# Ten of sixteen normalized tiles turned by DMA, the bias row loaded early, and eight banks for the first sums

## The chip, the cores and the metric

One core of one Trainium2 chip. The metric is the device time of one execution in microseconds (us), which is what all times below are. The matmul engine TensorE is called PE, VectorE DVE, ScalarE ACT, GpSimd POOL; SP issues most of the DMA transfers (in the kernel before all but 17 of the listed issues; the page lists no busy time for it).

A line of the profile's page called PEclk gives the clock granted to PE in tenths of full speed. Each execution also has a mean granted clock. In the profiled executions of the two kernels half clock (0.50) comes in stretches of 3.4 us or of twice that (in the kernel before from 50.3 to 57.1); both have a mean of 0.979. One stretch of 3.4 us takes about 0.011 off the mean (half of 3.4 is 1.7 us, of a span of 157 to 164), so by this estimate a mean of 1.000 says "no such stretch", 0.989 "one", 0.979 "two, or one of double length". This reading turns out to matter. An execution counts as slow here when it is over 1.5% above the fastest of the same kernel in its group of runs, otherwise as fast; only fast ones enter the ratios.

## The reference

```python
x  = A_x                                   # 1 x 2048 x 640, bf16
xn = layernorm(x)                          # over the 640
A  = irfft2(rfft2(xn) * (w_r + 1j * w_i))  # filter weights: 2048 x 321 each
B  = gelu(xn @ w1 + b1) @ w2 + b2          # w1 640 x 1536, w2 1536 x 640
return x + A + B
```

Two branches start from xn. The spectral one (A) is built from small matmuls with tables, of lengths 128, 16 and 160. The dense one (B) multiplies the transposed xn (xnT) with w1.

## The kernel before

The kernel is a list of operations with priorities; a scheduler in the program places them on engines by an estimate of their times, and the resulting order per engine is fixed at build time. Waits between engines are semaphores. Names that the argument needs: `xn` is a normalized tile of 128 rows (16 tiles in 8 pairs); `T` in the profile is the buffer that holds it; `ps` is PSUM, of which the program uses eight banks; `gT` the activated first-layer result; `gtab`, `etab`, `getab`, `htab`, `mtab`, `ntab` are tables; `Wf` holds the filter weights; `W` in the profile is w1 or w2: matmuls of `xnT,W` read w1, those of `W,gT` read w2 (W2 in the text), and of the loads `W<-in_B_w_dram` the ones after the first 10 us are those of W2. (DVE's `W` is an output buffer.)

How a tile was turned: five PE transposes into PSUM, then a copy. `BYDMA` is empty, so the DMA branch was not used:

```python
BYDMA = ()
...
if c in BYDMA:
    K.op([("sp", 1.6)], 0, lambda ...: e.dma_start_transpose(
         xnT[:, :, 128*c:128*c+128], xnv(n, 0, [[1, D]])), reads=[B_xn, xn], writes=[B_xnT[c]], ...)
    continue
tps = Buf(f"tps{c}", psum, 1, ZONE["tps"])
def xt(e, _, ...):
    for j in range(5):
        ins = e.transpose(psb(tps.slot, ...)[:, 128*j:128*j+128], xnv(n, 128*j, [[1, 128]]), ident[:])
...
K.op([("dve", 0.41), ("act", act_us(640))], pr, copy(... xnT <- tps ...))
```

SP's loads, in the order in which they were issued (the order of the text, which the scheduler in the program kept for SP):

```python
# x tiles, w1, tables G, E, M, N  [cut]
for ri, wsrc in enumerate((A_w_r, A_w_i)):      # 34 filter pieces
    ...  load_w(wsrc, p0, off, m1, 8, 1)  ...
load(W2[:], w2v, B_w2, F * D * 2)               # 1920 KB, one load
load(getab[:], const["GE"], B_ge, 204800)
load(htab[:]..., const["H"], B_h, 524288)
load(b2bc[:], ... b2 broadcast to 128 partitions ..., B_b2b, 163840)   # last
```

The program makes an instruction on SP wait for its inputs before it is issued, and everything behind it on SP waits too:

```python
for o in self.order[name]:
    for d in o.waits:
        e.wait_ge(d.sem, d.count)
    ins = o.emit(...)
```

## Time and profile before

| | before, profiled execution | before, other executions |
|---|---|---|
| time | 162.6 | 158.38, 159.2, 160.29 |
| span of the core | 160.8 | – |
| mean granted clock | 0.979 | not used in the prediction; see the experiments |
| PE busy | 148.7 (92%) | |
| PE's longest wait | 3.91, on activations behind the bias row b2bc | |

The last two rows are read in the prediction, with their lines. What the prediction does not show is where SP put W2, the second layer's weights. This is the timeline of SP in the kernel before (start, length, engine, line, operation, how many):

```profile
36.43 0.59 SPq L469 DMA_DIRECT2D W<-in_B_w_dram  x1
```

W2 is first read by PE at 60.04. It was issued 23.6 us ahead of need; the reader should keep that number.

### The profile page before, as it was taken

The numbers are of one execution on the slowest core, as the hardware profiler recorded it, in microseconds if no ns is written. First come the engines' busy times: TensorE is split into PE (matmuls) and PEld (weight loads), VectorE is DVE, ScalarE is ACT, GpSimd is POOL, SyncE is SP. The second block draws the span as 40 slices with busy tenths as digits, with TensorE's granted clock in tenths as the row PEclk, the third lists the DMA queues.
The fourth block names the chain that finished last, engine by engine and source line by source line (L and its number), as shares of the span: only waits on it lengthen the run. The fifth ranks groups of instructions, "written<-read, shape, count | busy, mean of one in ns | idle before, by whom it ended". The sixth has DMA issues, their size and how long they took to land.

```text
span 160.8 us, 4316 instructions
## 1 busy us (share of the span) xinstructions
PE 148.7 (92%) x1823; PEld 98.4 (61%) x1845; DVE 113.2 (70%) x258; ACT 84.0 (52%) x147; POOL 26.2 (16%) x33
## 2 busy tenths in 40 slices
PE   7979999999981999998999999998999999999994
PEld 7969899999850356464465355443447664665563
DVE  1659999999993024589995786991206999998222
ACT  3288989899709655353246884356865451211000
POOL 1112101111027600302113045202006000000000
PEclk9999999999997589999999999999999999999999
DMA  5999995458941940051649509996651914222112
GB/s 143 356 380 394 212 140 121 105 128 202 378 189 20 207 99 4 4 84 34 131 81 161 90 4 156 208 166 126 138 115 18 167 64 161 86 86 82 41 56 66
DMA packets 30394, 21.71 MB, mean 135 GB/s; under 512 B 12712, under 2 KB 28200, under 8 KB 30376
## 3 DMA queue, kind: packets, MB, share of 16 engines
q1 hardware_dynamic: 23320, 15.39, 38.4%
q0 software_dynamic: 6400, 5.24, 20.2%
q10 hardware_dynamic: 656, 0.82, 1.4%
q8 instruction: 14, 0.23, 0.6%
q14 instruction: 4, 0.03, 0.1%
HBM read 13.58 MB, written 2.62 MB: 101 GB/s over the span
## 4 chain that ended last, share of the span: by engine, by line
PE 57%; SPq 22%; DMA 8%; DVE 4%; ACT 4%; issue 3%; DVEq 0%
PE ps L474 57%; SPq L469 22%; DMA b2bc<-in_B_b_dram 6%; DVE T L723 2%; DMA XV<-U 2%; ACT gT L656 2%; ACT Wf L485 1%; DVE Z L727 1%; ACT xnT L803 1%; DVE Y L486 1%; DVEq L359 0%; ACT U L485 0%; DVE X L824 0%; DVE W L835 0%; SPq L748 0%
## 5 line engine op out<-in xcount | busy, mean ns | idle before, releaser
L474 PE MATMUL ps<-xnT,W 128*128 128x256 bf16 (+2 forms) x413 | 57.8, 294 | 6.0 <-ACT gT L656 4.6
L474 PE MATMUL ps<-W,gT 128*128 128x128 bf16 (+3 forms) x382 | 55.2, 292 | 1.6 <-issue 1.3
L474 PEld LDWEIGHTS ps<-xnT,W 128*128 128x128 bf16 x420 | 35.8, 99 | 23.2 <-ACT gT L656 6.3
L656 ACT ACTIVATE gT<-ps,b1col 128x256 bf16<-128x256 f32 (+2 forms) x84 | 39.7, 506 | 8.8 <-PE ps L474 6.8
L474 PEld LDWEIGHTS ps<-W,gT 128*128 128x128 bf16 x396 | 29.8, 98 | 23.3 <-issue 2.4
L826 POOL DMA_DIRECT2D xnT<-in_A_x_dram x8 | 12.3, 1785 | 33.0 <-ACT xnT L803 23.5
L567 DVE BATCH_NORM_STATS2 stats<-X 128x6 f32<-128x320 bf16 x32 | 14.3, 472 | 2.9 <-DMA X<-in_A_x_dram 2.9
L485 ACT ACTIVATE Wf<-ps 128x960 bf16<-128x960 f32 (+1 forms) x9 | 7.6, 878 | 15.5 <-PE ps L474 15.5
L723 DVE TENSOR_TENSOR T<-Y,Wf 128x1288 bf16<-128x1288 bf16 x16 | 12.4, 821 | 0.8 <-issue 0.8
L572 POOL TENSOR_TENSOR rstd<-ve,mhalf 128x2 f32<-128x2 f32 (+1 forms) x9 | 6.3, 699 | 38.1 <-DVE ve L571 38.1
L485 ACT ACTIVATE Xb<-ps 128x960 bf16<-128x960 f32 (+1 forms) x7 | 7.9, 1157 | 8.0 <-PE ps L474 7.8
L826 POOL DMA_DIRECT2D X<-in_A_x_dram x8 | 7.0, 873 | 27.1 <-DVE X L824 25.6
L485 ACT ACTIVATE XV<-ps 128x1280 bf16<-128x1280 f32 (+1 forms) x8 | 9.3, 1157 | 2.9 <-PE ps L474 2.7
L835 DVE TENSOR_TENSOR W<-ps,xnT 128x640 bf16<-128x640 f32 x8 | 6.5, 819 | 5.6 <-PE ps L474 5.4
L485 ACT ACTIVATE Y<-ps 128x644 bf16<-128x644 f32 x8 | 5.7, 707 | 8.5 <-PE ps L474 8.5
L486 DVE CAST Wf<-ps 128x960 bf16<-128x960 f32 (+1 forms) x3 | 3.1, 1044 | 8.6 <-PE ps L474 8.6
L486 DVE CAST Y<-ps 128x644 bf16<-128x644 f32 x8 | 6.6, 825 | 3.6 <-PE ps L474 3.6
L622 DVE TENSOR_TENSOR T<-T 128x512 bf16<-128x512 bf16 (+1 forms) x32 | 8.5, 315 | 0.0
L486 DVE CAST Xb<-ps 128x960 bf16<-128x960 f32 (+1 forms) x5 | 5.5, 1098 | 4.1 <-PE ps L474 4.1
L485 ACT ACTIVATE U<-ps 128x512 bf16<-128x512 f32 (+1 forms) x12 | 4.6, 435 | 7.1 <-PE ps L474 4.6
L835 DVE TENSOR_TENSOR W<-ps,X 128x640 bf16<-128x640 f32 (+2 forms) x10 | 6.7, 683 | 1.9 <-PE ps L474 1.9
L474 PE MATMUL ps<-getab,XV 32*128 32x160 bf16 (+1 forms) x128 | 7.6, 242 | 0.0
(47 smaller groups left out, 147.7 us busy)
## 6 DMA issues: line engine op xcount, KB each, us to landing
xnT<-in_A_x_dram POOLq DMA_DIRECT2D x8, 320.0 KB, 4.9
X<-in_A_x_dram POOLq DMA_DIRECT2D x8, 320.0 KB, 5.1
out_dram<-W SPq DMA_DIRECT2D x15, 160.0 KB, 1.8
X<-in_A_x_dram SPq DMA_DIRECT2D x7, 320.0 KB, 10.2
W<-in_B_w_dram SPq DMA_DIRECT2D x1, 1920.0 KB, 9.7
Wf<-in_A_w_r_dram SPq DMA_DIRECT2D x15, 80.2 KB, 9.3
Wf<-in_A_w_i_dram SPq DMA_DIRECT2D x15, 80.2 KB, 2.6
W<-in_B_w_dram ACTq DMA_DIRECT2D x1, 800.0 KB, 5.2
```

The lines of the kernel that those rows point to most:

```text
L469: return K.op([(q, 0.45)], 400, lambda e, _: e.dma_start(dst, src), reads=reads, writes=[buf], after=after, nbytes=nbytes, rate=rate)
L474: ins = e.matmul(o_, lhsT=lw, rhs=rh, start=st, stop=sp_, skip_group_check=True)
L485: return e.activation(dst(), src(), ACT.Copy, scale=scale)
L486: return e.tensor_copy(dst(), src())
L567: K.op([("dve", 0.393)], pr, lambda e, _, c=c, h=h: e.bn_stats(stats[:, c, 6 * h:6 * h + 6], view(X, c * D + H2 * h, [[1, H2]])), reads=[B ...
L572: K.op([("pool", 0.65)], pr, lambda e, _, a=a, b=b: e.tensor_tensor(out=rstd[:, a:b], in0=ve[:, a:b], in1=mhalf[:, a:b], op=ALU.pow), read ...
L622: ring_ops.append(K.op([("dve", dve_us(4 * w, 2))], pr, lambda e, _, op=op, x1v=x1v, xfv=xfv, o_=o_, o0=o0, o1=o1, w=w: e.tensor_tensor(ou ...
L656: K.op([("act", act_us(128 * nt, 1))], pr + PRIO["gelu"], lambda e, _, c0=c0, nt=nt, fc=fc, hps=hps: e.activation(gT[:, fc, 128 * c0:128 * ...
L723: filt_ops.append(K.op([("dve", dve_us(4 * KP, 2))], pr, lambda e, _, k=k, Y=Y, TB=TB, pair=pair: e.tensor_tensor(out=view(TT, TB.slot * 8 ...
L727: K.op([("dve", dve_us(2 * KP, 2))], pr, lambda e, _, TB=TB, Z=Z, r=r, op=op: e.tensor_tensor(out=view(Zb, Z.slot * 4 * KP + r * KP, [[2 * ...
L826: K.op([("pool", 1.5)], 51, lambda e, _, c=c, xov=xov, shaped=shaped: e.dma_start(xov(0, D), shaped(xv[:, c, :]), accum_op=ALU.add), reads ...
L835: K.op([("dve", dve_us(w))], 95, lambda e, _, os_=os_, fps=fps, o0=o0, w=w, xov=xov, shaped=shaped, base=base: e.tensor_tensor(out=shaped( ...
```

## The change

Its intent: take transposes off PE and their copies off DVE, close the hole at 48 to 52 us, and let the first sums use all eight banks. To get the DMA transposes out in time, SP may now take its loads by estimated time instead of by place in the text. The core of the diff:

```diff
-                if e == "sp":
-                    t, o = min(cands, key=lambda c: c[1].seq)
-                    if o is not min((p for p in pend[e] if not p.done), key=lambda p: p.seq):
-                        continue
-                else:
-                    t0 = min(c[0] for c in cands)
-                    ...
+                t0 = min(c[0] for c in cands)
+                ...
-BYDMA = ()
+BYDMA = tuple(range(6, 16))
+WLATE = (9.0, 0.9)
+W2LATE = (30.0, 4.0)
+EARLY = 4
@@ loads
+        load(b2bc[:], ..., B_b2b, 163840)             # now ahead of the filter pieces
-                 B_w, 16 * 642 * n, after=[wpad], rate=165e3)
+                 B_w, 16 * 642 * n, after=[wpad], rate=165e3, late=WLATE[0] + WLATE[1] * len(B_w.writers))
-        load(W2[:], w2v, B_w2, F * D * 2)
-        load(getab[:], const["GE"], B_ge, 204800)
-        load(htab[:]..., const["H"], B_h, 524288)
-        load(b2bc[:], ..., B_b2b, 163840)
+        for j in range(4):
+            load(W2[:, 3*j:3*j+3, :], w2v[:, 3*j:3*j+3, :], B_w2, 3*128*D*2, late=W2LATE[0] + W2LATE[1] * j)
+        load(getab[:], const["GE"], B_ge, 204800, late=60.0)
+        load(htab[:]..., const["H"], B_h, 524288, late=62.0)
@@ first-layer sums
-                hps = Buf(f"hps{bi}_{fc}", psum, 1, ZONE["hps"])
+                hps = Buf(f"hps{bi}_{fc}", psum, 1, ZONE["hps"] + (ZONE["bps"] if bi < EARLY else []))
```

The `late` values are hints to the scheduler (not before this time by its own estimate); no wait of the hardware comes from them. All four pieces of W2 write one buffer, `B_w2`, so the first product that reads W2 waits for all four.

More of the change, by code (lines that the diff above doesn't have):

```diff
@@ L248, in schedule @@
                     continue
-                if e == "sp":
-                    t, o = min(cands, key=lambda c: c[1].seq)
-                    if o is not min((p for p in pend[e] if not p.done), key=lambda p: p.seq):
-                        continue
-                else:
-                    t0 = min(c[0] for c in cands)
-                    near = [c for c in cands if c[0] <= t0 + 0.03]
-                    if e == "pe" and self.mode != "128":
-                        near = [c for c in cands if c[0] <= t0 + HOLD and c[1].alts and c[1].alts[0][0][0] == self.mode] or near
-                    t, o = min(near, key=lambda c: (-c[1].prio, c[1].seq))
+                t0 = min(c[0] for c in cands)
+                near = [c for c in cands if c[0] <= t0 + 0.03]
+                if e == "pe" and self.mode != "128":
+                    near = [c for c in cands if c[0] <= t0 + HOLD and c[1].alts and c[1].alts[0][0][0] == self.mode] or near
+                t, o = min(near, key=lambda c: (-c[1].prio, c[1].seq))
                 if best is None or t < best[0]:
@@ L466, in bass_parallel_sum__spectral_gfnet__dense_activation_gelu__prompt_kernel, with load @@
         p_yo, p_y2, p_yf, p_os = Pool(2), Pool(1), Pool(2), Pool(4)
-        def load(dst, src, buf, nbytes, after=(), reads=(), rate=395e3, q="sp"):
-            return K.op([(q, 0.45)], 400, lambda e, _: e.dma_start(dst, src), reads=reads, writes=[buf], after=after, nbytes=nbytes, rate=rate)
+        def load(dst, src, buf, nbytes, after=(), reads=(), rate=395e3, q="sp", late=0.0):
+            return K.op([(q, 0.6 if buf is B_w else 0.45)], 400, lambda e, _: e.dma_start(dst, src), reads=reads, writes=[buf], after=after, nbytes=nbytes, rate=rate, late=late)
         def mms(lst):
@@ L529, in bass_parallel_sum__spectral_gfnet__dense_activation_gelu__prompt_kernel @@
         load(ntab[:], const["N"], B_n, 49152, rate=70e3)
+        load(b2bc[:], bass.AP(tensor=b2v.tensor, offset=b2v.offset, ap=[[0, 128], [1, D]]), B_b2b, 163840)
         WP = 32 * KP
@@ L547, in bass_parallel_sum__spectral_gfnet__dense_activation_gelu__prompt_kernel @@
                             load_w(wsrc, p0 + 1, off + 2 * KP, 127, 7, -1)
-        load(W2[:], w2v, B_w2, F * D * 2)
-        load(getab[:], const["GE"], B_ge, 204800)
-        load(htab[:].rearrange("p a b -> p (a b)"), const["H"], B_h, 524288)
-        load(b2bc[:], bass.AP(tensor=b2v.tensor, offset=b2v.offset, ap=[[0, 128], [1, D]]), B_b2b, 163840)
+        for j in range(4):
+            load(W2[:, 3 * j:3 * j + 3, :], w2v[:, 3 * j:3 * j + 3, :], B_w2, 3 * 128 * D * 2, late=W2LATE[0] + W2LATE[1] * j)
+        load(getab[:], const["GE"], B_ge, 204800, late=60.0)
+        load(htab[:].rearrange("p a b -> p (a b)"), const["H"], B_h, 524288, late=62.0)
         B_b1ps, B_b1c = Buf("b1ps", psum), Buf("b1col")
@@ L599, in bass_parallel_sum__spectral_gfnet__dense_activation_gelu__prompt_kernel @@
                 if c in BYDMA:
-                    K.op([("sp", 1.6)], 0, lambda e, _, c=c, n=n, xnv=xnv: e.dma_start_transpose(xnT[:, :, 128 * c:128 * c + 128], xnv(n, 0, [[1, D]])),
-                         reads=[B_xn, xn], writes=[B_xnT[c]], nbytes=163840, rate=150e3)
+                    K.op([("sp", 1.25)], 500, lambda e, _, c=c, n=n, xnv=xnv: e.dma_start_transpose(xnT[:, :, 128 * c:128 * c + 128], xnv(n, 0, [[1, D]])),
+                         reads=[B_xn, xn], writes=[B_xnT[c]], nbytes=163840, rate=180e3)
                     continue
@@ L747, in bass_parallel_sum__spectral_gfnet__dense_activation_gelu__prompt_kernel @@
                     q = 2 * pair + qq
-                    K.op([("sp", 1.3)], 0, lambda e, _, q=q, qq=qq, U=U, uv=uv: e.dma_start_transpose(
+                    K.op([("sp", 1.25)], 500, lambda e, _, q=q, qq=qq, U=U, uv=uv: e.dma_start_transpose(
                         XV[:, :, 128 * q:128 * q + 128], uv(U, D * qq, [[1, D]])), reads=[U, B_u], writes=[B_v[q]], nbytes=163840, rate=180e3)
```

## The prediction

> **What bounds the kernel now.** I read the page's slices first, then the chain of work that ended last, then the timeline around the hole that these two point at, and last a table of stretches in the steady part before it.
>
> The slices (one digit is the busy share of 4.02 us; the third line is the granted TensorE clock):
>
> ```profile
> PE   7979999999981999998999999998999999999994
> DVE  1659999999993024589995786991206999998222
> PEclk9999999999997589999999999999999999999999
> DMA  5999995458941940051649509996651914222112
> ```
>
> The reader is to see that PE is at nine tenths nearly everywhere: the kernel is bound by TensorE, so that time is won only by taking work off PE or by filling its holes. There is one hole, in slices 12 and 13 (48 to 52 us, digits 8 and 1), and the clock falls to 7, 5, 8 right there and nowhere else.
>
> The chain, at that place (start, length, what):
>
> ```profile
> 37.06 0.91 SPq L469
> 37.97 0.04 issue
> 38.01 0.48 SPq L469
> 38.53 9.79 DMA b2bc<-in_B_b_dram
> 48.34 0.74 ACT xnT L803
> 49.08 0.58 ACT gT L656
> ...
> 51.49 6.30 PE ps L474 x23
> ```
>
> Everything before 38.5 us in this chain is SP issuing one load after another; the broadcast bias row b2bc is the last of SP's 55 loads. It takes 9.79 us to land, ACT waits for it, the activations queued on ACT behind it wait with it, and PE waits for those. The timeline gives the sizes (last bracket: idle before, and what ended it):
>
> ```profile
> 48.34 0.74 ACT L803 ACTIVATE xnT<-b2bc 128x640 f32<-128x640 bf16 x1 [4.44 <-DMA b2bc<-in_B_b_dram]
> 51.49 5.73 PE L474 MATMUL ps<-xnT,W 128*128 128x512 bf16 x13 [3.91 <-ACT gT L656]
> 57.02 0.78 PE L474 MATMUL ps<-gtab,T 128*128 128x128 bf16 x10
> ```
>
> PE is idle for 3.91 us. The table of stretches shows what it costs afterwards (PE busy with its count, granted clock, DMA share, GB/s):
>
> ```profile
> 50.65:57.05 6.40, 5.56 (x14) 0.50 1.05 154
> ```
>
> The 13 matmuls of 512 columns start at 51.49 and the next group at 57.02: 5.53 us, 0.425 us each. In the fast part (34 such matmuls from 112.50 to the next group at 120.06) one takes 0.222 us. The half clock so costs 5.53 - 13 x 0.222 = 2.6 us on top of the 3.9.
>
> The steady part before the hole (PE, PEld, DVE, ACT, POOL, clock, DMA share, GB/s):
>
> ```profile
> 30.70:35.90 5.20, 5.20 (x60) 4.78 (x58) 5.20 (x19) 4.50 (x9) 0.69 (x1) 1.00 0.48 112
> ```
>
> 5.2 us is the period of one pair of x tiles. PE and DVE are both full, and ACT is at 4.5 of 5.2. The DMA rings are half used, while SP is issuing filter weights at about 0.6 us each.
>
> [...] 3.91 us idle, then 0.50 from 50.65 to about 57.0. [...] the activations behind the bias copy stood still for 4.44 us although the sums they were to read had been finished. [...] b2bc, 160 KB, took 9.8 us behind 1920 KB of W2 and 512 KB of H; the transposes that the kernel already makes land in 2.6/3.3/7.4 us (least, median, most). [...] Here a DMA transpose does five blocks at once for about 1.3 us of SP's time (medians 1288 to 1906 ns), and five blocks on PE take 0.28 us plus a copy of 0.48 us on DVE.
>
> **The change part by part.**
>
> Bias row early: no instruction is added; one load of 0.53 us moves from place 55 to just before the filter weights. It would be issued near 9.8 us instead of 38.5 and land long before ACT wants it at 44. Both the hole (3.9 us) and the half clock after it (2.6 us) should go: 6.5 us, all on PE, all on the path.
>
> Ten tiles turned by DMA: it takes 50 transposes off PE. From the timeline a pair's ten start at 31.32 and the next group at 31.88: 0.56 us a pair, five pairs, 2.8 us off the bounding engine. It also takes ten copies xnT<-ps off DVE: a pair's two cost 0.89 us, so 4.4 us in all, and DVE's period falls from 5.2 to about 4.3 us from the fourth pair on. It adds ten DMA transposes to SP: 10 x about 1.3 = 13 us of issuing. SP now issues from 9.8 to 36.4 the 34 filter pieces, 26.6 us; with the ten the stretch ends about 13 us later, near 50, and filter weights are first read at 69 (perhaps 59 after the change). So SP's work stays hidden, narrowly. The transposes' latency of about 3 us, 7 at worst, replaces about 1.5 us of PE transpose plus copy. The first sums lag behind the normalization: the 512-column sums of tiles 8 to 11 start about 44 us, while tile 11 was normalized at about 36. Eight microseconds of slack; hidden.
>
> Eight banks for the first four blocks of sums: PE waited 0.70 us for ACT at 9.64 us with all four banks full. More banks let it run on; ACT is the bound there (8.57 of 10 us in 10 to 20), so I count 0.5 us.
>
> W2 in four pieces, E and H tables late: bytes are unchanged, first use of W2 is 60 us. I count 0.
>
> Sum in the profiled execution: 3.9 + 2.6 + 2.8 + 0.5 = 9.8 us of 160.8. As PE is full elsewhere and its remaining work is the same, work put off from the early part (the first sums, whose share in the shorter pair period shrinks) fills later places, where PE would otherwise have waited or done the same work anyway.
>
> **The rivals.**
>
> (a) The hole is smaller outside the profile. The profiled execution took 162.6 us and the three others 158.38 to 160.29, median 159.2: 3.4 us less. If that difference sits in the landing of b2bc[...], only 9.8 - 3.4 = 6.4 us are there to win: 152.8. If the profile stretches all evenly, it is 159.2 x (1 - 9.8/160.8) = 149.5. The spread of 1.9 us among the three speaks for a part that varies; nothing in one profile decides it.
>
> (b) SP or the DMA rings become the wait. The transposes stand in order with filter pieces whose landing takes up to 12 us early on (the stretch at 0 to 20 us has DMA shares of 0.86 and 1.09), and each waits on SP for its normalization, holding what follows it. Against it: by 25 us, when the first is issued, the later filter pieces land in 2.6 us and the share is 0.5. Should one miss, PE loses 1 to 3 us: 152 to 154. [...]
>
> (c) ACT becomes the bound. With a pair period of 4.3 us ACT has 1.24 us of XV copy and needs 0.49 us for each 256-column activation, while PE makes one such sum in 0.54 us. In 4.3 us ACT can serve 6.2 sums, which with the 0.56 us of PE's own G product keeps PE busy 3.9 of 4.3 us. That could cost up to 0.4 x 4 = 1.6 us. But the scheduler may hand XV copies to the relieved DVE. I count it as part of the range.
>
> (d) The middle chain (width transform, filter, inverse, turned by SP) does not follow. Its start, the last G product, moves from 57.0 to about 46. PE has first and second layer work to fill it, as now (PE waits of 0.1 to 0.5 us between 60 and 120). If the chain stretched to its old end, the gain would be only some 3 us: 156. Against it, DVE, its other engine, has about a fifth of its time free between 60 and 110.
>
> **Range and chances.** The mean of the two readings of (a) is 151.2; I predict 151.3 us. Low end: all of 9.8 and a bit of the clock's variation, 148.3. High end: the smaller hole and 2 us of (b) or (c), 154.8. The 2% line is 156.0. To miss it, (b) or (d) must take nearly everything; I give 0.07 to within 2% and 0.01 to slower, 0.92 to faster.
>
> **What would show it.** In the profile after: no ACT wait on b2bc and no clock digit below 9 after the start; 30 PE transposes instead of 80, 6 copies xnT<-ps instead of 16; a DVE pair period of 4.2 to 4.5 us from about 25 us; the last G product at 46 to 48 us; PE's busy time some 5 us lower (2.8 of transposes, 2.6 of slow clock), and no PE wait over 1 us from 10 us on. Wrong would be: PE waiting for an xnT transpose or on activations held up by another load; SP reaching the last filter piece after the first filter product wants it; a second drop of the clock; or a before-kernel that shows no hole when not profiled, so that the gain is 3 us short.

## The result

| | before | after |
|---|---|---|
| median of the four runs of each taken side by side | 158.79 (156.84 to 160.29, 4 runs) | 162.62 (162.60 to 165.45, 4 runs) |
| ratio of fast runs | 1 | 1.0306 (95%: 1.0209 to 1.0404): slower |
| mean clock of the runs | not on record for these four; 1.000 in most others (see e5) | 0.979, in one of six 0.989 |
| profiled execution: span | 160.8 | 163.7 |
| profiled execution: PE busy / idle | 148.7 / 12.1 | 146.6 / 17.1 |

The ratio here and below is the mean time of one kernel's fast runs over that of the other's fast runs of the same rounds, so it is not quite the ratio of the two medians. Predicted were 151.3 us and a gain; the kernel lost 3%. Both profiled executions are slow ones of their kernel with the same mean clock, 0.979. They are compared below to find the places where time goes; what each place costs in fast runs is taken up with the experiments.

The slices of the kernel after (one digit for 4.09 us; PE, DVE, granted clock, DMA):

```profile
PE   7979999989899819999999999999199959999994
...
DVE  1659999999932574489669859552067899598222
...
PEclk9999999999999996999999999999959999999999
DMA  5999996969999990052773799599800772302112
```

The hole at 48 to 52 us is gone, but there are two new ones: slices 13 and 14 (counted from 0; 53 to 61 us, digits 8 and 1) and slice 28 (115 to 119 us, digit 1). After each of them the clock dips (6; 5). The DMA line stands at 9 from slice 9 to slice 14 (37 to 61 us) and falls to 0 when the first hole ends, so transfers were under way all through it. The waits of PE (total, times, longest) name the two holes:

```profile
PE ps L472 <- DMA W<-in_B_w_dram: 3.9, 1, 3.9
...
PE ps L472 <- DMA XV<-U: 3.3, 1, 3.3
...
PE ps L472 <- DVE W L834: 1.6, 1, 1.6
```

The first waits for W2. Why W2 is late stands in SP's timeline after:

```profile
10.61 11.91 SPq L467 DMA_DIRECT2D Wf<-in_A_w_r_dram  x17
22.57 1.16 SPq L467 DMA_DIRECT2D Wf<-in_A_w_i_dram  x1
26.10 2.62 SPq L599 DMA_TRANSPOSE xnT<-T  x2
28.76 2.54 SPq L467 DMA_DIRECT2D Wf<-in_A_w_i_dram  x4
...
47.33 2.70 SPq L599 DMA_TRANSPOSE xnT<-T  x2
50.07 1.87 SPq L467 DMA_DIRECT2D Wf<-in_A_w_i_dram  x3
51.99 2.19 SPq L467 DMA_DIRECT2D W<-in_B_w_dram  x4
```

From 26.1 to 54.2 us SP is never free: ten transposes (15.3 us together, 1.3 to 2.5 each) and 16 filter pieces (10.1 us, about 0.6 each) alternate, and W2 stands behind all of them. Before that SP stood idle from 23.7 to 26.1, because the first transpose waits for its tile to be normalized (DVE normalizes the pair from 25.63 to 26.43, the transpose is issued at 26.10). W2 is issued at 51.99, where before it was issued at 36.43: 15.6 us later. The scheduler in the program had put these four loads at 47.3 to 48.6 and their landing at 54.0 by its own estimate. The chain of work that ended last (start, length, what) shows the landing, and the same pattern at the second hole:

```profile
53.69 6.88 DMA W<-in_B_w_dram
...
60.61 4.62 PE ps L472 x36
...
113.82 4.75 DMA XV<-U
...
118.61 1.23 PE ps L472 x14
```

PE's timeline after (last bracket: idle before, and what ended it) gives the sizes, and one prediction that came true:

```profile
47.45 0.72 PE L472 MATMUL ps<-gtab,T 128*128 128x128 bf16 x10
...
60.61 2.84 PE L472 MATMUL ps<-W,gT 128*128 128x512 bf16 x12 [3.86 <-DMA W<-in_B_w_dram]
...
118.61 1.23 PE L472 MATMUL ps<-getab,XV 128*128 128x160 bf16 x16 [3.29 <-DMA XV<-U]
```

The last G product starts at 47.45, where it started at 57.02 before: 9.6 us of lead, as the prediction wanted (46 to 48). Then PE reaches the first product with W2 at 60.61 - 3.86 = 56.75, and stands. The table of stretches for what follows the two holes (length; PE busy and count, PEld, DVE, ACT, POOL; clock, DMA share, GB/s):

```profile
60.61:66.80 6.19, 6.03 (x48) 3.87 (x50) 2.67 (x6) 1.52 (x2) 0.00 (x0) 0.72 0.10 38
...
118.61:123.50 4.89, 4.55 (x44) 3.08 (x45) 2.61 (x5) 1.39 (x2) 0.00 (x0) 0.65 0.00 0
```

6.03 us busy at a clock of 0.72 are 6.03 x 0.28 = 1.7 us lost; 4.55 us at 0.65 are 1.6 us. So the balance between the two profiled executions closes:

| term of PE's time | us |
|---|---|
| hole of the bias row gone: idle / half clock after it | -3.9 / -2.6 |
| 50 transposes gone | -2.8 |
| wait for W2: idle / half clock after it | +3.9 / +1.7 |
| wait for the last XV transposes: idle / half clock | +3.3 / +1.6 |
| wait for DVE W, late | +1.6 |
| sum | +2.8 |
| measured, 163.7 - 160.8 | +2.9 |

The gain came, 9.3 us of it; new waits, two of them of the same two-part kind as the one removed, took back 12.1. This is the balance of two slow executions. The fast runs differ by more (1.0306 is some 4.8 us), because the usual execution of the kernel before has less of the hole that was removed (e5).

### The profile page after: what moved, and what is told of

It reads as the page before. It is cut to its first block, busy times and chain, and to the rows that moved or that the text cites. A ratio compares the mean times of both kernels' runs of the same rounds, so it can differ in the third digit from the quotient of the medians.

```text
span 163.7 us, 4234 instructions
## 1 busy us (share of the span) xinstructions
PE 146.6 (90%) x1774; PEld 96.5 (59%) x1795; DVE 111.8 (68%) x252; ACT 80.8 (49%) x143; POOL 26.2 (16%) x33
## 2 busy tenths in 40 slices
DMA packets 37162, 23.35 MB, mean 143 GB/s; under 512 B 19480, under 2 KB 34968, under 8 KB 37144
## 4 chain that ended last, share of the span: by engine, by line
PE 74%; DMA 11%; ACT 4%; DVE 3%; SPq 3%; issue 3%; DVEq 0%; ACTq 0%
PE ps L472 73%; DMA XV<-U 5%; DMA W<-in_B_w_dram 4%; DMA xnT<-T 2%; SPq L467 2%; ACT gT L655 1%; PE ps L606 1%; ACT L655 1%; ACT XV L483 1%; DVE W L834 1%; SPq L747 1%; ACT Wf L483 1%; DVE XV L484 1%; DVE U L484 1%; SPq L599 1%
## 5 line engine op out<-in xcount | busy, mean ns | idle before, releaser
L472 PE MATMUL ps<-W,gT 128*128 128x512 bf16 (+3 forms) x385 | 56.9, 296 | 6.5 <-DMA W<-in_B_w_dram 3.9
L472 PE MATMUL ps<-xnT,W 128*128 128x256 bf16 (+2 forms) x411 | 56.5, 288 | 3.5 <-ACT gT L655 1.1
L472 PEld LDWEIGHTS ps<-xnT,W 128*128 128x128 bf16 x420 | 34.6, 98 | 18.3 <-issue 2.8
L655 ACT ACTIVATE gT<-ps,b1col 128x256 bf16<-128x256 f32 (+2 forms) x84 | 38.6, 509 | 10.3 <-PE ps L472 9.2
L483 ACT ACTIVATE Wf<-ps 128x960 bf16<-128x960 f32 (+1 forms) x8 | 6.8, 870 | 23.2 <-PE ps L472 23.2
L483 ACT ACTIVATE Xb<-ps 128x960 bf16<-128x960 f32 (+1 forms) x8 | 8.7, 1121 | 12.9 <-PE ps L472 12.7
L825 POOL DMA_DIRECT2D X<-in_A_x_dram x8 | 8.0, 996 | 30.6 <-DVE X L823 29.5
L484 DVE CAST Wf<-ps 128x960 bf16<-128x960 f32 (+1 forms) x4 | 4.3, 1072 | 8.7 <-PE ps L472 8.7
L472 PEld LDWEIGHTS ps<-getab,XV 32*128 32x128 bf16 (+1 forms) x128 | 6.9, 147 | 5.3 <-DMA XV<-U 3.8
L823 DVE TENSOR_TENSOR X<-ps,b2bc 128x640 f32<-128x640 f32 x7 | 5.7, 817 | 3.7 <-PE ps L472 3.7
```

Of the source, the lines that this page charges most:

```text
L472: ins = e.matmul(o_, lhsT=lw, rhs=rh, start=st, stop=sp_, skip_group_check=True)
L483: return e.activation(dst(), src(), ACT.Copy, scale=scale)
L484: return e.tensor_copy(dst(), src())
L655: K.op([("act", act_us(128 * nt, 1))], pr + PRIO["gelu"], lambda e, _, c0=c0, nt=nt, fc=fc, hps=hps: e.activation(gT[:, fc, 128 * c0:128 * ...
L823: kept_ops.append(K.op([("dve", dve_us(D))], 30, lambda e, _, kps=kps, xov=xov, shaped=shaped: e.tensor_tensor(out=xov(0, D), in0=shaped(p ...
L825: K.op([("pool", 1.5)], 51, lambda e, _, c=c, xov=xov, shaped=shaped: e.dma_start(xov(0, D), shaped(xv[:, c, :]), accum_op=ALU.add), reads ...
```

## The experiments

Two theories stand. (I) SP's in-order issuing: the ten transposes, with their issue time and their waits for normalized tiles, push W2 (and what else is behind them) past its need; remedy that, and the predicted gain is there. (II) The DMA engines: the transposes, and the accumulating loads that the early bias row moved to 27 to 46 us, fill the DMA engines (their share in 20 to 50 us is 1.02 in the kernel after, 0.67 in the kernel before), so that W2 would be late wherever SP issued it. A third question is what the bias row's hole was worth in executions that were not the slow profiled one.

### e1: only the bias row early, on the kernel before

```diff
+        # SP's order: the load of b2bc ahead of the first filter piece; all else as it was
+        sp = K.order["sp"]; moved = [o for o in sp if B_b2b in o.writes]; ...
+        K.order["sp"] = rest[:at] + moved + rest[at:]
```

> The kernel before with one thing changed: SP issues the bias row ahead of the filter pieces; the order on every other engine is the same. My theory of the hole in the kernel before (3.9 us idle and 2.6 us at half clock, all from that one load): no idle time over 1 us on TensorE near 48 us, no clock below 1.0 there, and 6.5 us less, a ratio of 0.96 (152 us). Rival 1, the hole is mostly an effect of profiling: about 3 us less, 0.98. Rival 2, what is filled there is lost later, as the changed kernel suggests: within 1 us of the kernel before, 1.00.

Measured: 155.49 (155.44 to 155.77), ratio 0.9887 (0.9854 to 0.9919), mean clock 1.000 in all four. No wait of PE over 1.0 us is left in the profile: SP issues the row early, and PE runs its 13 matmuls without the wait and at full clock (SP's timeline, then PE's):

```profile
9.36 0.54 SPq L469 DMA_DIRECT2D b2bc<-in_B_b_dram  x1
```

```profile
47.34 2.98 PE L474 MATMUL ps<-xnT,W 128*128 128x512 bf16 x13
```

So the mechanism is right: one load moved closes the hole. But the gain is 1.1%, some 1.8 us, not 6.5. The same kernel was run again later, on another chip (e14):

> The kernel before with only the bias row moved, once more on the same chip as the two runs before it, to compare them: 155.5 us, ratio 0.989, clock 1.000.

gave 155.45 (155.37 to 155.73), ratio 0.9862 (0.9825 to 0.9900).

### e5: the kernel before once more

Unchanged, for a profile of an undisturbed execution.

> The kernel before, unchanged, for another look with the profile: of seven runs of it beside the last experiments five had a mean clock of 1.000 and two had 0.989. If the run is one of the common kind: TensorE still waits for the bias row near 48 us, [...] with no drop of the clock, and the span is 155 to 156.5 us instead of 160.8. If the profile itself makes the long wait, the look again shows 3.9 us, a clock of 0.98 and 160 us.

Measured: 158.56, clock 1.000, span 156.7. PE's timeline, then ACT's:

```profile
49.99 3.15 PE L474 MATMUL ps<-xnT,W 128*128 128x512 bf16 x13 [2.42 <-ACT gT L656]
```

```profile
46.84 0.74 ACT L803 ACTIVATE xnT<-b2bc 128x640 f32<-128x640 bf16 x1 [2.95 <-DMA b2bc<-in_B_b_dram]
```

The hole is there but 2.42 us long, not 3.91, and the 13 matmuls after it take 52.98 - 49.99 = 2.99 us, 0.23 each: full clock. Of the 44 runs of the kernel before that were timed beside the experiments, 34 have a clock of 1.000 (one 0.999) and 156.93 to 158.58 us, nine 0.989 and 159.38 to 160.69, and one 0.979 and 162.04. The groups differ: beside e12 to e14 all seven have 1.000, beside e9 to e11 only three of seven. The profile that the prediction was made from, with 0.979, was the exception, and so the sum of 6.5 us priced a rare execution. In the usual one the hole costs about 2 us, which the two runs above show.

### e2: the four W2 loads moved ahead of the transposes of tiles 12 and 13

```diff
+        # after the schedule: SP's loads that write W2 go in front of the transpose of tile 12
+        moved = [o for o in sp if B_w2 in o.writes]; at = <first that writes B_xnT[12]>
+        K.order["sp"] = rest[:at] + moved + rest[at:]
```

> The changed kernel with the four W2 loads moved on SP ahead of the transposes of tiles 12 and 13; every other engine's order is the same. Theory: the wait of 3.86 us at 56.7 us and its half clock (about 1.7 us) go, the wait at the start of the last stage stays: 5.6 us less than the changed kernel, about 157 us, ratio 0.99. Rival, the middle chain or the width of the other work sets the end: the wait goes and the end hardly moves, 161 to 163 us, ratio 1.02 to 1.03.

Measured: 163.31 (160.05 to 164.56), three of four runs in the slow state, so no ratio. W2 was issued from 41.01, and the first product with it runs at 56.02 without a wait. PE waits later instead:

```profile
PE ps L472 <- DVE xnT L823: 4.3, 1, 4.3
```

The last filter pieces were issued from 55.31 here, and DVE, which multiplies with them, stands still for them. The kernel of e4 has the same order on SP and shows it plainly, in DVE's timeline:

```profile
61.36 2.31 DVE L723 TENSOR_TENSOR T<-Y,Wf 128x1288 bf16<-128x1288 bf16 x3 [4.19 <-DMA Wf<-in_A_w_i_dram]
```

The two transposes just behind W2 in SP's order took 4.19 us to issue (from 44.69), against 2.6 to 3.8 for a pair in the kernel after. What follows: the expectation that W2's wait was a matter of one load's place was wrong. What stood behind W2 was late in its stead.

### e3: the accumulating loads of tiles 10 and 11 held until the last transposes of the middle chain have landed

The second hole needs its own test. After the change, POOL issued accumulating loads at 110.42 and 113.68, beside the last four XV transposes, which landed in 3.8 to 4.9 us; before, with none beside them, they took 2.6 to 2.7 each.

```diff
-  reads=[xb2], writes=[xo], nbytes=327680, rate=150e3)
+  reads=[xb2], writes=[xo], nbytes=327680, rate=150e3, after=v_ops if c in (10, 11) else [])
```

> The changed kernel with the accumulating loads of x tiles 10 and 11 held back until the last DMA transposes have landed; the order on every engine is the same. Theory: they slow the last four transposes (3.8 to 4.9 us to landing each, against 2.6 in the kernel before, where none runs beside them); held back, the four land in 2.6 to 2.8 us, the wait of 3.3 us at the start of the last stage and its half clock (1.5 us) shrink to under 1 us: 3.5 to 4.8 us less, 158 to 159 us, ratio 1.00. Rival, the transposes are slow of themselves or late because the work ahead of them is: they still take about 4 us, and no change within 1 us, 1.03.

Measured: 160.98 (159.91 to 161.70), ratio 1.0225 (1.0162 to 1.0288), clock 0.989 in the profile, span 159.0. The last four transposes land in 2.7 us each, and the group that waited 3.29 us no longer does:

```profile
115.50 1.07 PE L472 MATMUL ps<-getab,XV 128*128 128x160 bf16 x16
```

The wait for W2 stays, at 3.8. The profiled span fell by 4.7 us, about the hole and its half clock (3.3 + 1.6); the timed median fell by only 1.6, between different groups of runs, and the two intervals overlap (1.0162 to 1.0288 against 1.0209 to 1.0404). So that the wait goes is shown; what it costs in fast runs is not. These have spans of 160.1 to 160.8 in the kernel after, against its profiled 163.7, at the same mean clock; no trace of one exists, so where they are shorter stays open.

### e4: both

The edits of e2 and e3 in one kernel.

> Both edits of the two runs before it at once. Theory: the two waits are separate and their savings add, 9 to 10.4 us less than the changed kernel: 152 to 154 us, ratio 0.96 to 0.97. Rival, one wait hides another (the accumulates then come at other times): only the larger of the two savings, 157 us, 0.99.

Measured: 159.99 (159.32 to 161.50), ratio 1.0181 (1.0104 to 1.0258). PE's longest wait is 4.2, on DVE, behind the filter weights (the line above). Still 1.8% slower than before.

### e6: the change without its ten DMA transposes

```diff
-BYDMA = tuple(range(6, 16))
+BYDMA = ()
```

> The changed kernel with one constant set back: no normalized tile is turned by DMA; early bias row, eight banks, SP by time and the late loads stay. Theory (the ten transposes fill SP's queue and so push W2 and the filter weights past the time they are wanted): SP is done with the filter weights by about 40 us, no wait for W2, a clock near 1.0, 154 to 156 us, ratio 0.98 to 0.99. Rival (the loss comes from the other parts: the late loads, the order made for eight banks): the wait for W2 or another of over 3 us stays and the ratio is over 1.01.

Measured: 156.22 (155.74 to 158.02, 20 runs), ratio 0.9912 (0.9883 to 0.9940), clock 1.000, no PE wait over 1.0 us. SP is early again; this is its last W2 piece:

```profile
39.01 0.61 SPq L467 DMA_DIRECT2D W<-in_B_w_dram  x1
```

This is the experiment that puts the loss on the transposes: with them 1.0306, without 0.9912, a difference of 0.039 or some 6 us (the two ratios are from different groups of runs, each against the kernel before). The rest of the change (early row, eight banks, W2 in pieces) gives no more than the early row alone did. The eight banks were not run by themselves, so their predicted 0.5 us is neither shown nor refuted; the two ratios, 0.9912 against 0.9887 and 0.9862, leave no room for a gain from them beside the others.

### e7 and e8: W2 issued by POOL instead of SP

```diff
+        # the four W2 loads leave SP; POOL issues one after each of its 4th to 7th rstd
+        w2s[n_r - 4].eng = "pool"; new.append(w2s[n_r - 4])
```

> The changed kernel with the four W2 loads issued by GpSimd after its fourth to seventh rstd, so that neither W2 stands behind SP's queue nor the filter pieces behind W2; the other engines' orders are the same. Theory, SP's issuing is what is short: the filter weights are all issued 2 us earlier than in the changed kernel, no wait for W2 and none for filter weights, 5 to 6 us less than the changed kernel, 157 us, ratio 1.00. Rival, the DMA engines themselves are full from 20 to 55 us (their share is 0.9 to 1.1 in the changed kernel): the filter weights then land later by what W2 takes, the first filter product waits 3 us or more, and the time is as in the run where W2 went earlier on SP, 160 to 163 us.

> The same with the accumulating loads of tiles 10 and 11 held back until the last transposes have landed. Theory: both large waits gone, clock near 1.0, 152 to 155 us, ratio 0.97 to 0.985. Rival (DMA engines full): 158 to 161 us, ratio 1.00 to 1.02.

Measured: 172.77 (166.58 to 174.37; three of four runs slow, no ratio), and with the accumulates of tiles 10 and 11 held as well 168.33 (165.86 to 168.69; two of four slow, no ratio). Even the fastest runs, 166.58 and 165.86, are longer than those of the kernel after. Both are the opposite of what theory I expected. Now the transposes themselves are late; SP's timeline and PE's:

```profile
31.68 7.26 SPq L599 DMA_TRANSPOSE xnT<-T  x2
```

```profile
37.65 3.36 PE L472 MATMUL ps<-xnT,W 128*128 128x256 bf16 x15 [4.74 <-DMA xnT<-T]
```

Two transposes took 7.26 us to issue, where a pair took 2.6 to 3.8 in the kernel after; they land in up to 15.4 us (2.7 to 6.1 there). With POOL as a second issuer the transposes landed later, not sooner: this fits theory II, as far as the transposes go. It needn't be the issuer that hurts: here W2 is issued at 19.4 to 34.2 us, in the middle of the transposes, and e2, where W2 came from SP itself, shows slow transposes behind it too (4.19 us of issue for the pair). The two changes weren't taken apart.

### e9: 34 filter pieces as 8 loads of the same bytes

The same rows and bytes, with nearly as many packets (36746 against 37162), in fewer instructions. The rows come to the wrong places, so the result is wrong on purpose.

```diff
+        # every group of four or five pieces becomes one load of 512 rows of 642 bytes
+        K.order["sp"] = [o for o in K.order["sp"] if o not in gone]
```

> The changed kernel, its 34 filter pieces replaced by 8 loads of as many rows and bytes (4096 rows of 642 bytes), spread over the same places in SP's order; the rows land in other places, so the result is wrong on purpose. Every other engine's order is the same. It takes 26 issues, at least 15.6 us, off SP and nothing off the DMA engines. If SP's issuing is what is short: W2 is issued by about 46 us instead of 52, lands by 53, the wait for W2 is gone, 3.5 to 5.6 us less than the changed kernel, 157 to 159 us. If the DMA engines are what is short: the transposes take longer to issue and land (over 2 us and over 5 us in the middle), W2 still lands at 58 us or later, and the wait stays above 2 us: 161 to 163 us.

Measured: 159.27 (158.82 to 160.62), ratio 1.0067 (0.9973 to 1.0160), in a noisy group (the fast runs of the kernel before average 158.4 here and about 157.6 beside the other experiments; against those the ratio would be about 1.012). SP's timeline and PE's:

```profile
47.05 2.97 SPq L467 DMA_DIRECT2D W<-in_B_w_dram  x4
```

```profile
58.05 1.80 PE L472 MATMUL ps<-W,gT 128*128 128x512 bf16 x12 [2.03 <-DMA W<-in_B_w_dram]
```

W2 is issued 4.9 us earlier and lands 2.6 earlier (58.0 against 60.56); the wait falls to 2.03 us, the other one to 2.2, and neither is followed by half clock (this trace has no clock record, but the 12 matmuls take 1.80 us here and 2.84 in the kernel after): the mean clock is 1.000 in two of the four runs and 0.989 in two, where the fast runs of the kernel after had 0.979 or, once, 0.989. The ratio falls from 1.0306 to 1.0067. Of the profiled span's 6.4 us some 3.5 come from the first hole with its half clock and 2.7 from the second. So removing instructions from SP, at equal bytes, takes away most of the loss, as theory I has it. But the run does not go all its way: the landing at 58 us and a wait just above 2 us had been written down for theory II. Two things in the trace say why.

First, the 12 pieces taken out after 26 us free 7.7 us of issuing, yet W2 is issued only 4.9 earlier. SP now stands idle in front of transposes, 4.3 us in all (for instance from 29.25 to 30.29), until their tiles are normalized, and the last transpose is issued at 44.5. W2 behind ten transposes waits for the tenth tile, however few the pieces. Second, W2 landed only 2.6 us earlier for 4.9 of issue: its landing was longer (11 us from the first issue, 8.6 in the kernel after), so the time of issue is not all of it. What made it longer was not shown.

### e10: early accumulating loads held until W2 has landed

```diff
-  reads=[xb2], writes=[xo], nbytes=327680, rate=150e3)
+  reads=[xb2], writes=[xo], nbytes=327680, rate=150e3, after=B_w2.writers if c in HOME[:5] else [])
```

> The changed kernel with the four accumulating loads that it makes between 27 and 46 us held back until W2 has landed; SP's, PE's, DVE's and ACT's orders are the same. It takes 1.3 MB of accumulating traffic out of the stretch and no issue off SP. If the DMA engines are what is short: the ten transposes land in about 3 us instead of 4.3 (median), SP reaches W2 2 us or more earlier, the wait for W2 is 2 us or less, 2 to 4 us less than the changed kernel. If SP's issuing is: W2 is issued at 51 to 52 us as before, the wait stays near 3.5 us, within 1 us of the changed kernel, or worse, since the held loads now meet the later transposes.

Measured: 162.84 (161.02 to 165.14), ratio 1.0188 (1.0059 to 1.0316). The DMA engines are relieved: their share in 20 to 50 us falls from 1.02 to 0.75, and the transposes land in 2.7/2.7/3.9 us (least, median, most) instead of 2.7/4.3/6.1. The edit did less than the expectation says: three of the four loads were held (POOL issues them from 59.56), the fourth, of an `X` tile, went out at 44.70, so it is 1.0 MB and not 1.3. It hardly helps W2: the product that waits for it starts at 59.31 instead of 60.61. SP's timeline and the wait of PE:

```profile
51.09 2.19 SPq L467 DMA_DIRECT2D W<-in_B_w_dram  x4
```

```profile
PE ps L472 <- DMA W<-in_B_w_dram: 3.8, 1, 3.8
```

Beside e9 this separates the theories for the issue of W2: fewer instructions at the same traffic bring it 4.9 us forward, less traffic at the same instructions only 0.9. It does not separate them for W2's landing, which took 8 to 11 us in all three kernels.

### e11: only tiles 12 to 15 turned by DMA

```diff
-BYDMA = tuple(range(6, 16))
+BYDMA = tuple(range(12, 16))
```

A wait of the filter on these transposes was added, because with this order it could have overwritten a buffer that a transpose still read.

> The changed kernel with only tiles 12 to 15 turned by DMA (and the filter made to wait for these transposes, which the check asks for here). W2 is issued in SP's order ahead of or among them, and 13 us of SP's issuing becomes 5. Theory (SP and the DMA engines were full only because of all ten): no wait for W2, clock 1.0, TensorE has 1.1 us less to do than without any: 155 to 156 us, ratio 0.98 to 0.99, at or just under the run with none. Rival (any DMA transpose among these loads costs more than it saves): 157 us or more.

Measured: 157.32 (156.99 to 158.13), ratio 0.9937 (0.9858 to 1.0016), clock 1.000, no wait for W2. Four fit on SP, and gain nothing over none (0.9912).

### e12: room made for all ten: 8 filter loads, W2 ahead of the first transpose, accumulates held

The edits that helped SP and the last stage, together (wrong result on purpose, because of the 8 loads).

> The changed kernel with 8 filter loads in place of 34 (wrong result on purpose), W2 on SP ahead of the first transpose, and the accumulating loads of tiles 10 and 11 held: all that is thought to be short is given at once, and the ten DMA transposes stay. The orders of PE, DVE and ACT are the changed kernel's. Theory (the transposes themselves pay once SP has room, and the two waits were all the loss but 1.6 us): no wait for W2, filter weights or the last transposes over 1 us, clock 1.0, 163.7 - 5.6 - 4.8 in the profile, 152 to 155 us, ratio 0.97. Rival 1 (the ten transposes cost by themselves, through the DMA engines): transposes land in over 5 us, TensorE waits for xnT or DVE for the buffers of the normalized tiles, 157 us or more.

Measured: 155.24 (154.85 to 155.65), ratio 0.9846 (0.9797 to 0.9895), clock 1.000. SP has room:

```profile
18.54 3.41 SPq L467 DMA_DIRECT2D W<-in_B_w_dram  x4
```

PE's longest wait is the 1.6 on DVE, and the transposes, landing in 2.6/4.7/6.4, hold nobody up. The loss is gone. But in the same group the kernel before with nothing but the early bias row made 0.9862: even when the transposes hold nobody up, this version is 0.2 us ahead of that one, well inside the intervals, where the 50 transposes off PE should have brought 2.8. Of theory I the part about the loss so holds, the part about the predicted gain does not. The 1.6 us wait on DVE W, which the kernels with ten DMA transposes show and those with none or four do not, eats part of the 2.8. What causes it was not tested.

### e13: the same with correct filter weights: 17 pieces moved to POOL

```diff
+        # the 17 pieces of w_i leave SP; POOL issues three after each rstd from the second on
+        # W2 ahead of the first transpose, accumulates held, as above
```

> A version with right results that gives SP room: of the changed kernel, the 17 pieces of the imaginary filter weights go to GpSimd's queue behind its rstd instructions, W2 stands on SP ahead of the first transpose, the accumulating loads of tiles 10 and 11 are held. Theory (SP's issuing): as the run before it, 152 to 155 us, under the 155.5 us of the kernel before with only the bias row moved. Rival (a second queue of small descriptors beside the transposes slows these, as W2 on GpSimd did): transposes issue in over 2 us, DVE waits for their buffers, 160 us or more.

Measured: 170.15 (169.65 to 171.88), ratio 1.0811 (1.0742 to 1.0880). SP's timeline, and the wait of PE:

```profile
28.52 30.13 SPq L599 DMA_TRANSPOSE xnT<-T  x10
```

```profile
PE ps L472 <- DMA xnT<-T: 13.8, 1, 13.8
```

Now SP has nothing else to do, and it does not help. The ten transposes, behind W2 in SP's order, take 1.2/1.4/6.0 us to issue and 2.6/3.3/17.6 to land (least, median, most), and PE, which waits for one of them, goes on at 46.90. Whether the cause is POOL's transfers sharing the engines or W2 just ahead in SP's own queue (in the run before, W2 was issued 6.6 us earlier than here, at 18.54) is not settled: the two were changed together.

No correct version with the ten DMA transposes beat the kernel before. The best correct one is the kernel before with its bias row moved, 155.45.

## Why the prediction was wrong

**"Bias row early: ... 6.5 us".** Mechanism right, size wrong. No wait on b2bc is left, and the clock dip behind it is gone. In the usual execution the hole is 2.42 us and is not followed by half clock, and the row alone is worth 1.1 to 1.4%, about 2 us. The prediction's rival (a) named this ("The hole is smaller outside the profile") and the result follows it; its 3.4 us were even short of the 4.5 that were missing. The profile's own mean clock of 0.979 could have decided it, had the clocks of more runs of the kernel before been known.

**"2.8 us off the bounding engine".** Right as a count: PE has 30 transposes instead of 80, there are 6 such copies instead of 16 (5 instead of 15 of them on DVE), and PE's busy time fits (the balance above). Right also in effect up to 47 us: DVE's work for a pair comes every 4.3 us, as predicted (4.2 to 4.5), and the G products, less evenly, at 4.4, 5.0, 4.4, 5.1 and 2.7 us, on average 4.3 ((47.45 - 25.93)/5). What it is worth at the end of the run is another matter: e12 shows 0.2 us beyond the bias row.

**"W2 in four pieces, E and H tables late: bytes are unchanged, first use of W2 is 60 us. I count 0."** and **"SP's work stays hidden, narrowly."** This is the step that failed. The prediction worked out that SP's stretch would end "near 50", and it did (the last filter piece at 51.3). It then compared this with the first use of the filter weights alone, 59 us. But W2 stands behind the filter pieces. Its issue moved to 51.99 to 54.2 and its landing to 60.56, while its first use moved forward from 60.04 to 56.75 because PE gained time, as wanted. The numbers were in reach: W2 had been issued at 36.43 and had landed 9.7 us later; with 13 us of transposes ahead of it that makes 36.4 + 13 + 9.7 = 59.1, and PE, 5 us or more ahead of its old times, would want it well before. The cost, 3.9 idle and 1.7 at half clock, is the old hole at another place. The experiments confirm the cause: without the transposes the wait is gone; with fewer instructions on SP it halves; with less accumulating traffic it stays; and moving W2 forward hands it to the filter weights, so that the place of W2 alone is not the matter. How much of the late landing belongs to SP's order and how much to the filled DMA engines stays open.

**"Rival (b) ... 152 to 154".** Right mechanism, wrong load and size. It thought of transposes and filter pieces, not of W2 behind them. It let one miss of 1 to 3 us happen. There were two, of 3.86 and 3.29 us, both with half clock after them in the profiled run.

**"The middle chain follows" (rival (d) denied).** Half right. Its work came forward (the last products with ntab from 112.05 to 107.01), but its last XV transposes met accumulating loads that had not been beside them before, and the products after them waited 3.29 us. Holding two accumulates removes the wait: shown. The timed medians differ by 1.6 us there, which is not clear of noise.

**"No PE wait over 1 us from 10 us on".** False in three places: 3.9, 3.3 and 1.6.

**"0.01 to slower".** Far too sure. All 9.8 us were counted as won on PE; of the loads that moved, only one deadline was checked.

## What to carry to other kernels

When work is moved to an issuer that runs in order, as SP does here (behind ten transposes and 16 filter pieces W2 was issued at 51.99 us, not at 36.43), add up its whole queue, issue time by count, waits for inputs and landing, and compare it with the deadline of everything behind, taking the deadlines of the faster kernel, not those of the old one. Before a hole is priced from a profile, look at the clock and time of several runs: here a profile in the slow state showed a hole with its half clock, where 34 of 44 runs of the same kernel have a clock of 1.000. And take a bundle apart: here one moved load had the whole gain, and the ten transposes cost three times as much as that load won (some 6 us against 2).
